# A hand-written order of stages for five queues, replaced by another order of the same stages

## The chip, the cores and the metric

The kernel runs on one core of a Trainium2 chip. The metric is the device time of one execution in microseconds (us); the median of several executions is compared. PE is TensorE (matmuls), DVE is VectorE, ACT is ScalarE, POOL is GpSimd, and SP is the queue that issues every DMA transfer here.

## What is computed

Sliding-window attention with 32 global tokens, then two feed-forward layers in a row, all in float32. Cut to what matters:

```python
# attention: B=4 batches, H=8 heads, 512 local + 32 global tokens, head size 64
s_g = scale * q_g @ concat(k_g, k_l).T          # global queries see everything
out_g = softmax(s_g) @ concat(v_g, v_l)
s_l = concat(q_l @ k_g.T, where(|i - j| <= 32, q_l @ k_l.T, -1e9)) * scale
out_l = softmax(s_l) @ concat(v_g, v_l)
x = concat(out_g, out_l)                        # as 2304 tokens x 512

h = x @ w_in                                    # first FF layer, 512 -> 1024
solu = h * softmax(h)
ln = (solu - mean) / sqrt(var + 1e-6) * g_ln
x = ln @ w_out                                  # 1024 -> 512

h = x @ w_in2                                   # second FF layer, 512 -> 2048
g = where(h >= 1, h, where(h <= -1, 0, (h + 1)**2 / 4))
out = g @ w_out2                                # 2048 -> 512
```

Each float32 matmul of the FF layers is done as three fast ones on a high and a low part of both operands (`mm3`, and `hmm` with its `lo` argument). The weights come as 64-bit words and are turned into these two parts on the chip, in the steps A, C, B, D, F, m, H, L of `conv`.

## The kernel before, in words

The 2304 tokens are 18 tiles of 128 at most; attention and the first FF layer go through 16 tiles of local tokens and one of all global ones, in the order `SEQ`, step by step. The second FF layer follows behind for three blocks of tiles, 16 steps each, and is not touched.

The first eight steps (`SCRIPTED = 8`) are not written as a loop but as one list of short names, `SCRIPT`. A loop takes the names one after the other, and `issue` emits the instructions of each. All five engines are in a manual schedule there, so each engine's queue holds its instructions just in the order of the list; across engines only data, buffers and semaphores set the time. A name is a kind and a step or piece number, and a trailing `v` puts it on DVE in place of ACT or POOL:

- loads, on SP: `q` (qkT, queries and keys of a step), `v` (vw, the value windows), `qg`, `vn` (for the global tokens), `w` (a raw piece of the first layer's weights);
- attention of a step: `S` scores and `G` global scores on PE, `M`, `R`, `Rn` edge mask, row maximum and its scale on DVE, `Ea`, `Eb` exponentials on ACT, `Ta`, `Tb` transposes on PE to pPT and `Pa`, `Pb` their copies, `V` the product with vw on PE (tile o, called pv here), `X` its scaling (xn), `XT` the transposition into the tile xy; `gt`, `gp`, `gv` and so on the same for the global tokens, once in four steps;
- first FF layer of a step: `xh`, `xl` high and low part of x, `ha`, `hA`, `hb`, `hB` the matmuls to h (a step has 24), `mx`, `ex`, `z`, `u`, `bn`, `pw`, `nn` softmax and normalization (`u` is the multiplication e<-e,s,h which reads h a last time), `ta`, `tb`, `tha`, `tla` and so on the transposes to lnT, `ya`, `Ya`, `yb`, `Yb` the matmuls to yT (24 each, for two steps at once);
- weight pieces: `A` to `L`, as above; pieces 16 to 18 belong to the second layer's weights, are stored to memory for later (`s` fetches one, `o` stores one);
- `Z`: three matmuls on a tile of zeros that keep PE occupied (`keep_warm`).

Buffers that bind steps: psH (2 rooms for S and h), psA (3 rooms for transposes, o and others), 2 rooms each for qkT and vw, 3 for raw weights (wraw). A load into a room waits on SP until its last reader is done, and everything behind it on SP waits too.

Behind the list the loop `for p in range(SCRIPTED, NT)` goes on with step 8. Its first pass runs, by `ORDER_1 = "h3x0421g5w"`: h of step 8, the rest of step 11's attention, x of the next step, the transposes of step 12 (pPT), two sets of yT, pv of step 12, and then the scores of step 14.

Of the kernel before, what the change touches and what calls it, by code (L numbers as in the profile page):

```python
# [49 lines left out]
SCRIPTED = 8  # L50

SCRIPT = """
Z0 Z0 Z0 q0 Z0 qg0 w3 q1 A3 w0 S0 M0 Z0 C3 R0 B3 Z0 G0 D3 Gc0 S1 G1 w2 q2 Rn0 M1 F3 Ea0 w5 q3 H3 A0
Ta0 w4 Gc1v R1 Rn1 Eb0 A2 L3 S2 G2 Z0 C0 B0 C2v D0 B2 M2 Ea1 Eb1 F0 A5 C5 I1 D2 H0 R2 Gc2 L0v v0 Z0
Pa0 Tb0 A4 B5 Pb0 F2 G3 w1 H2 Rn2 Ta1 I0 L2 q4 v1 Gc3v qg1 V0 Ea2 C4v gm0 A1 B4 C1 gn0 D4 S3 q5 D5
Tb1 X0 Eb2 M3 R3 B1 Pa1 ge0 Rn3 F4 Z0 F5 Ea3 Z0 Pb1v D1 gt0 XT0 gp0 S4 H4 Ta2 Eb3 M4 L4 V1 gc0 H5
gi0 Tb2 Pa2 w7 L5 R4 Pb2 S5 I2 X1 w6 A7 G4 F1 Rn4 A6 Gc4 M5 Z0 H1 I3 G5 C7v XT1 R5 Z0 Ea4 B7 Gc5 v2
q6 v3 V2 L1 Rn5 xh0 Eb4 X2 C6 Ta3 Pa3v B6 D6 Ea5 Tb3 q7 XT2 S6 w8 F6 Tb4 M6 Pb3 D7 Eb5 Ta4 V3 ha0 H6
xh1 F7 X3 Pa4 Pb4 n0 xl0 L6 R6 A8v w10 H7 L7 G6 v4 Rn6 Gc6 XT3 A10v Ea6 hA0 G7 I4 hb0 q8 Ta5 hB0
Gc7v C10v Eb6 gm1 V4 mx0 C8 B10 ex0 Ta6 I5 xl1 Pa5 ha1 X4 hA1 B8 z0 gn1 D10 D8 I6 w9 F8 Tb5 u0 v5 m8  # L60
hb1 Pb5 F10 V5 XT4 hB1 xh2 bn0 H8 m10 vn0 L8 A9 C9 ge1 v6 mx1 S7 M7 pw0 q9 Pa6 X5 ex1 qg2 Tb6 R7 Pb6
Rn7 xh3 Ea7 w11 Eb7 z1 gv0 B9 H10 go0 gt1 u1 V6 D9 v7 xl2 S8 XT5 nn0 w13 ha2 gp1 X6 M8 R8 L10 A11
xl3 tb0 thb0 ta0 Rn8 tlb0 v8 Ea8 w12 hA2 I7 tha0 C11 Eb8 A13 Tb7 F9 hb2 Ta7 B11 w14 bn1 hB2 tla0 D11
Pa7v xh4 m9 pw1 Pb7 ha3 nn1 C13 tb1 B13 mx2 F11 hA3 qg3 w15 H9 ta1 thb1 tha1 m11 D13 ex2 tlb1 XT6
tla1 L9 z2 F13 H11 s0 hb3 gc1 m13 L11 V7 hB3 Ta8 H13 gi1 mx3 ex3 ya0 Pa8 u2 A12 X7 XT7 bn2 xl4 S9 z3
Tb8 G8 q10 L13 Ya0 A15 xh5 Pb8 M9 u3 ha4 C12 Gc8 A14 G9 Gc9 hA4 R9 C15 Rn9 B15 pw2 q11 G10 C14 B12
B14 D15 D12 Ea9 vn1 nn2 F12 Eb9 m12 H12 F15 yca0 hb4 tb2 I8 hB4 Gc10v ta2 bn3 L12v S10 mx4 V8 m15
D14 xl5 H15 thb2 tlb2 X8 ex4 z4 F14 s1 yb0 tha2 pw3 v9 u4 gv1 tla2 nn3 go1 ha5 s2 m14 M10 G11 Ta9
Pa9v H14 Gc11 R10 bn4 A16 L15 L14 Yb0 v10 ta3 tha3 tb3 hA5 A17v I9 thb3 Tb9 tla3 Rn10 C17 Ea10 hb5
tlb3 ycb0 C16v Ta10 A18 pw4 Eb10 XT8 hB5 ya1 gm2 xh6 mx5 Pb9v ex5 xl6 B16 z5 S11 nn4 u5 bn5 xh7 D16  # L70
M11 V9 B17 Ya1 D17 ha6 gn2 F17 X9 Pa10 F16 Tb10 pw5 Pb10 nn5 tb4 hA6 ta4 tha4 q12 R11 Rn11 yca1 hb6
q13 V10 ge2 yb1 I10 Ea11 xl7v tla4 XT9 thb4v X10 Eb11 tlb4 xd1 hB6 C18 mx6 xh8 B18 Yb1 ex6 z6 S12 u6
tb5 H17 XT10 Ta11 H16 Pa11v M12 thb5 tlb5 ha7 ta5 hA7 tha5v I11 bn6 tla5 ycb1 gt2 R12 Rn12 pw6 hb7
gp2 Ea12 G12 Gc12 gc2 hB7 Eb12 D18 Tb11 L17v ya2 Pb11v G13 nn6 mx7 F18 ex7 S13 Gc13v z7 u7 v11 M13
H18 bn7 L18 R13 L16 Rn13 o0 s3 V11 ta6 tha6 tb6 o1 Ya2 gi2 Ea13 tla6 thb6v Eb13 yca2 vn2 q14 v12
xl8v pw7 tlb6 v13 X11 xd0 I13 I12 nn7
"""

ROOMS = [2, 3, 4, 0, 1, None, None, None, 2, 3, 4, 0, 1, None, None, None]
# [911 lines left out]
```

## Time and profile before

| | |
|---|---|
| median of 3 executions | 704.96 us (704.93 to 706.45) |
| the profiled execution | 709.54 us, of which the span from the first to the last instruction is 707.7 us |
| PE busy in the span | 682.5 us (96%) |
| DVE busy | 421.2 us (60%) |
| ACT busy | 294.4 us (42%) |
| POOL busy | 178.4 us (25%) |
| transfers | 72.25 MB, on the mean 102 GB/s |

The busy shares are means over the whole span, and its parts have different limits. The written list takes PE from 0 to about 168 us, the loop goes on to about 315 us, and the second FF layer takes the rest. So what happens in the list is to be read from windows of the first 170 to 190 us, not from this table. A row of the timeline gives the start, the duration, the engine, the line and the operation with the tile it writes and those it reads, and in brackets how long the engine stood before it and what ended that.

### The profile page before, as it was taken

Reading aid. Unit: us, or ns where it says so; the run is one execution under the profiler, and the core shown is the slowest. Engines: PE = TensorE matmul, PEld = TensorE weight load, DVE = VectorE, ACT = ScalarE, POOL = GpSimd, SP = SyncE. Lnnn points to the kernel's source line nnn. Section 1 sums busy time; section 2 is a strip of 40 time slices with the busy share of each in tenths; the row PEclk is TensorE's granted clock in tenths of the full one; section 3 lists DMA queues with packets and bytes.
Section 4 is the critical chain, followed back from the end, with each engine's and each line's share of the span. In section 5 each row is a group of like instructions: output and inputs, shape, how many; then the busy total and the mean of one; then the engine's idle time right before and its main releaser. Section 6 shows DMA issues by size and latency. Waiting matters only on the chain.

```text
span 707.7 us, 14836 instructions
## 1 busy us (share of the span) xinstructions
PE 682.5 (96%) x6200; PEld 594.5 (84%) x6200; DVE 421.2 (60%) x777; ACT 294.4 (42%) x736; POOL 178.4 (25%) x188
## 2 busy tenths in 40 slices
PE   7889899999799999999999999999999999999997
PEld 3557788888789898899988889899998898999995
DVE  5989898988677569666977774432222243322232
ACT  5876663555346244443444442332222233222222
POOL 2234364103012114202313222222222222222210
PEclk9889999999899999999999999999999999999999
DMA  8978737303932813201322200020000002000002
GB/s 337 359 301 312 286 117 303 110 2 112 370 122 100 298 31 120 60 1 60 119 88 92 90 30 1 2 89 1 1 0 1 1 0 75 16 1 1 0 1 75
DMA packets 18162, 72.25 MB, mean 102 GB/s; under 512 B 2224, under 2 KB 2736, under 8 KB 15536
## 3 DMA queue, kind: packets, MB, share of 16 engines
q1 hardware_dynamic: 18096, 71.32, 27.8%
q8 instruction: 48, 0.79, 0.4%
q14 instruction: 18, 0.15, 0.1%
HBM read 63.71 MB, written 7.60 MB: 101 GB/s over the span
## 4 chain that ended last, share of the span: by engine, by line
PE 70%; DVE 16%; DMA 7%; ACT 4%; issue 3%; SPq 0%; ACTq 0%; DVEq 0%
PE acc L264 21%; PE h L264 20%; PE h L509 9%; PE yT L264 9%; DVE w L177 3%; DVE w L179 2%; PE S L340 2%; DMA wraw<-in_w2i_dram 2%; DMA wraw<-in_w2o_dram 2%; PE plnT L558 2%; PE o L412 2%; DVE nm L137 2%; ACT e L146 2%; DVE xy L137 1%; DMA vw<-in_vwin_dram 1%
## 5 line engine op out<-in xcount | busy, mean ns | idle before, releaser
L264 PE MATMUL h<-yT,w2i 128*128 128x384 f32 (+1 forms) x936 | 167.6, 328 | 2.3 <-DVE xy L137 2.3
L264 PEld LDWEIGHTS h<-yT,w2i 128*128 128x128 f32 x936 | 157.7, 188 | 10.0 <-DVE xy L137 3.8
L161 POOL TENSOR_TENSOR g<-xy,g 128x384 fp32r<-128x384 f32 (+1 forms) x92 | 91.8, 998 | 282.0 <-ACT g L146 262.0
L137 DVE TENSOR_SCALAR xy<-h 128x384 f32<-128x384 f32 (+1 forms) x96 | 51.2, 533 | 145.1 <-PE h L264 128.9
L264 PE MATMUL acc<-w2o,g 128*128 128x512 f32 x510 | 127.9, 394 | 0.0
L146 ACT ACTIVATE xy<-xy 128x384 f32<-128x384 f32 (+1 forms) x96 | 48.4, 504 | 145.8 <-DVE xy L137 145.8
L264 PEld LDWEIGHTS acc<-w2o,g 128*128 128x128 f32 x510 | 94.4, 188 | 17.2
L509 PE MATMUL h<-win,x 128*128 128x512 f32 x408 | 105.5, 405 | 0.4 <-DVE x L497 0.4
L264 PE MATMUL yT<-lnT,wout 128*128 128x256 f32 x768 | 95.1, 281 | 0.7 <-ACT xy L146 0.7
L264 PEld LDWEIGHTS yT<-lnT,wout 128*128 128x128 f32 x768 | 92.1, 188 | 2.1 <-ACT xy L146 0.9
L509 PEld LDWEIGHTS h<-win,x 128*128 128x128 f32 x408 | 74.1, 189 | 17.6 <-issue 1.4
L137 DVE TENSOR_TENSOR xy<-h,xy 128x384 f32<-128x384 f32 (+1 forms) x96 | 51.3, 534 | 56.9 <-ACT xy L146 56.8
L146 ACT ACTIVATE g<-xy 128x384 fp32r<-128x384 f32 (+1 forms) x96 | 48.7, 507 | 60.0 <-DVE xy L137 39.4
L146 ACT ACTIVATE e<-S,nm 128x128 f32<-128x128 f32 x128 | 45.3, 382 | 11.5 <-DVE nm L137 7.7
L264 PE MATMUL h<-yT,lnT 128*128 128x384 f32 (+1 forms) x216 | 38.8, 328 | 0.0
L264 PE MATMUL acc<-lnT,g 128*128 128x512 f32 x153 | 38.2, 393 | 0.0
L264 PEld LDWEIGHTS h<-yT,lnT 128*128 128x128 f32 x216 | 36.5, 188 | 2.0 <-DVE xy L137 0.5
L171 ACT ACTIVATE w<-wraw 128x512 f32<-128x512 f32 x37 | 24.8, 677 | 27.1 <-DMA wraw<-in_w2o_dram 14.6
L264 PEld LDWEIGHTS acc<-lnT,g 128*128 128x128 f32 x153 | 28.3, 188 | 5.1
L177 DVE SCALAR_TENSOR_TENSOR w<-wraw,w 128x512 int32<-128x512 int32 x38 | 32.1, 854 | 0.4
L497 POOL TENSOR_TENSOR x<-xy,x 128x512 fp32r<-128x512 f32 x15 | 20.0, 1335 | 45.3 <-ACT x L146 45.3
L137 DVE TENSOR_REDUCE nm<-h 128x1 f32<-128x1024 f32 x17 | 20.7, 1218 | 17.4 <-PE h L509 17.4
(120 smaller groups left out, 819.2 us busy)
## 6 DMA issues: line engine op xcount, KB each, us to landing
vw<-in_vwin_dram SPq DMA_DIRECT2D x16, 1024.0 KB, 9.6
qkT<-in_qk_dram SPq DMA_DIRECT2D x16, 832.0 KB, 5.2
wraw<-in_w2i_dram SPq DMA_DIRECT2D x16, 512.0 KB, 3.7
wraw<-in_w2o_dram SPq DMA_DIRECT2D x16, 512.0 KB, 3.7
vn<-in_vloc_dram SPq DMA_DIRECT2D x4, 1024.0 KB, 8.1
out_dram<-o SPq DMA_DIRECT2D x16, 256.0 KB, 2.0
xy<-in_w1i_dram SPq DMA_DIRECT2D x5, 512.0 KB, 8.9
xy<-in_w1o_dram SPq DMA_DIRECT2D x5, 512.0 KB, 8.6
```

Source lines behind the costliest of these rows:

```text
L137: self.last = getattr(nc.vector, name)(*args, **kw)
L146: vec.act = nc.scalar.activation(**kw)
L161: eng.tensor_tensor(out=lo, in0=src, in1=hi.bitcast(F32), op=ALU.subtract)
L171: return nc.scalar.activation(out=w.tf, in_=w.high.bitcast(F32), func=AF.Abs)
L177: return nc.vector.scalar_tensor_tensor(out=w.t, in0=w.high, scalar=-0x40000000, in1=w.t, op0=ALU.bitwise_and, op1=ALU.bitwise_or)
L179: return nc.vector.scalar_tensor_tensor(out=w.t, in0=w.low, scalar=29, in1=w.t, op0=ALU.logical_shift_right, op1=ALU.bitwise_or)
L264: mm(out=dst, lhsT=pairs[i][0][x], rhs=pairs[i][1][y], start=start and j == 0, stop=stop and j == 3 * n - 1)
L340: mm(out=S[32 * hp:32 * hp + 32, par, ci], lhsT=qT[r, hp, ci], rhs=kT[r, hp, w:w + 4].rearrange("p c d -> p (c d)"), start=True, stop=True)
L412: mm(out=o[rows, ci, par], lhsT=PT[t][:, par, ci, rows], rhs=w[:, ci, D * h:D * h + D], start=True, stop=True)
L497: eng.tensor_tensor(out=xT[t][1], in0=x[:, :, n:n + P], in1=xT[t][0].bitcast(F32), op=ALU.subtract)
L509: mm(out=hps[t][:, half], lhsT=x[i][:, k], rhs=win[j][:, k, sl], start=not lo and j == 0 and k == 0, stop=lo and k == KD - 1)
L558: nc.tensor.transpose(ps[:, k], ln[t][:, P * c:P * c + P], ident)
```

## The change

`SCRIPT` is written anew. The same stages are in it, with the same numbers, but in another order; `Z` stands there 3 times in place of 12. Some names change the engine by their `v` (for instance `Pa3v` to `Pa3`, `L6` to `L6v`): DVE has 736 rows in the new order and 744 in the old one, PE 2258 and 2314. The loop, the buffers and everything behind the list stay as they were.

```diff
 SCRIPT = """
-Z0 Z0 Z0 q0 Z0 qg0 w3 q1 A3 w0 S0 M0 Z0 C3 R0 B3 Z0 G0 D3 Gc0 S1 G1 w2 q2 Rn0 M1 F3 Ea0 w5 q3 H3 A0
-Ta0 w4 Gc1v R1 Rn1 Eb0 A2 L3 S2 G2 Z0 C0 B0 C2v D0 B2 M2 Ea1 Eb1 F0 A5 C5 I1 D2 H0 R2 Gc2 L0v v0 Z0
...
-H18 bn7 L18 R13 L16 Rn13 o0 s3 V11 ta6 tha6 tb6 o1 Ya2 gi2 Ea13 tla6 thb6v Eb13 yca2 vn2 q14 v12
-xl8v pw7 tlb6 v13 X11 xd0 I13 I12 nn7
+qg0 q0 w2 S0 w1 q1 M0 A2 w0 G0 C2 q2 R0 B2 Rn0 w3 D2 A1 v0 Ea0 Eb0 C1 F2 H2 w7 S1 B1 D1 L2 Gc0 Ta0
+F1 I0 A0 M1 C0 Pa0 Tb0 S2 R1 G1 B0 q3 D0 Rn1 H1 Pb0 A3 Ea1 Z0 Gc1 F0 C3 M2 V0 R2 B3 Rn2 H0 Ta1 D3 w6
...
+Eb12 Gc13v G12 H16 Gc12 S13 Tb11 Pb11 ya2 mx7 V11 nn6 tb6 L16v M13 ta6 vn2 R13 ex7 Rn13 z7 Ea13 tha6
+H18 xd1 u7 xl8 o0 Eb13 thb6 bn7 pw7 Ya2 L18 v13 nn7 s3 I13 o1 yca2 q14 XT10 tlb6 X11 gi2 I12 tla6
 """
```

Three places show what moved. The first is SP's queue at the end of the list, which feeds the loop's first pass. Before, from the vw of step 11 (vw_2697) to the vw of steps 12 and 13 (vw_2808 and vw_2813); w2d_i0 and w2d_i1 are the stores `o0` and `o1`, wraw_2715 is the fetch `s3`, vg and vn are `vn2`, qkT_2806 is `q14`:

```order
L318 DMA vw_2697<-in_vwin_dram 128x2048
L245 DMA w2d_i0_2713<-wraw_1545 128x1024
L233 DMA wraw_2715<-in_w2o_dram 128x1024
L245 DMA w2d_i1_2761<-wraw_1931 128x1024
L323 DMA vg_2803<-in_vglo_dram 32x512
L324 DMA vn_2802<-in_vloc_dram 128x2048
L314 DMA qkT_2806<-in_qk_dram 128x1664
L318 DMA vw_2808<-in_vwin_dram 128x2048
L318 DMA vw_2813<-in_vwin_dram 128x2048
```

Now, from the vw of step 11 (vw_2272) on; vw_2558 is that of step 12, vw_2766 that of step 13, qkT_2776 is `q14`:

```order
L317 DMA vw_2272<-in_vwin_dram 128x2048
L313 DMA qkT_2538<-in_qk_dram 128x1664
L317 DMA vw_2558<-in_vwin_dram 128x2048
L322 DMA vg_2704<-in_vglo_dram 32x512
L323 DMA vn_2703<-in_vloc_dram 128x2048
L244 DMA w2d_i0_2726<-wraw_1924 128x1024
L317 DMA vw_2766<-in_vwin_dram 128x2048
L232 DMA wraw_2769<-in_w2o_dram 128x1024
L244 DMA w2d_i1_2773<-wraw_1926 128x1024
L313 DMA qkT_2776<-in_qk_dram 128x1664
L313 DMA qkT_2834<-in_qk_dram 128x1664
```

The vw of step 12 moved from behind both stores to a place ahead of them and of vg and vn; the one of step 13 stands between the stores, and q14 is still behind the second.

The second place is PE's queue at the first matmul to h, the first work of the FF layer. Before, with the last of twelve keep-warm sets ahead of it:

```order
L270 MATMUL Z<-zero 128x512
L412 MATMUL o<-vw,PT 32x64 x32
L397 MATMUL pPT<-ident,e 128x128 x8
L340 MATMUL S<-qkT 32x128 x32
L397 MATMUL pPT<-ident,e 128x128 x8
L412 MATMUL o<-vw,PT 32x64 x32
L509 MATMUL h<-win_133,x 128x512 x4
L509 MATMUL h<-win_134,x 128x512 x4
```

Now:

```order
L269 MATMUL Z<-zero 128x512
L339 MATMUL S<-qkT 32x128 x32
L396 MATMUL pPT<-ident,e 128x128 x4
L411 MATMUL o<-vw,PT 32x64 x32
L396 MATMUL pPT<-ident,e 128x128 x4
L508 MATMUL h<-win_133,x 128x512 x4
L508 MATMUL h<-win_134,x 128x512 x4
```

Before, seven scores, six global scores, ten half transposes, four pv (o) and the transposes of the first global group stand ahead of the first h, with all twelve keep-warm sets; now five scores, four global scores, six half transposes and two pv, with three sets. The difference stands behind it.

The third place is DVE's queue at the end of the list, from the row maximum of h of step 7 (nm<-h) to the multiplication `u7` (e<-e,s,h), which frees the room of h. Before, with the normalization of step 6 (e<-e,mv,rstd) ahead of it:

```order
L137 TENSOR_SCALAR e_2457<-e_2457,mv,rstd 128x1024
L137 TENSOR_REDUCE nm_2653<-h 128x1
L179 SCALAR_TENSOR_TENSOR w_2131<-wraw,w_2131 128x512
L137 COPY Sg<-G 128x128 x2
L137 TENSOR_SCALAR s_2657<-s_2657 128x1
L137 RECIPROCAL s_2657<-s_2657 128x1
L137 SCALAR_TENSOR_TENSOR e_2656<-e_2656,s_2657,h 128x1024
```

Now:

```order
L136 TENSOR_REDUCE nm_2655<-h 128x1
L136 TENSOR_SCALAR e_2385<-e_2385,mv,rstd 128x1024
L184 TENSOR_TENSOR wraw<-w_1973,wraw 128x512
L136 TENSOR_TENSOR S<-S,masks 128x8x2x32
L136 TENSOR_REDUCE nm<-S 128x8
L136 TENSOR_SCALAR nm<-nm 128x8
L136 TENSOR_SCALAR s_2710<-s_2710 128x1
L136 RECIPROCAL s_2710<-s_2710 128x1
L136 STREAM_TRANSPOSE xy_90<-ogn 128x4x32
L136 SCALAR_TENSOR_TENSOR e_2709<-e_2709,s_2710,h 128x1024
```

The normalization of step 6, a low part of a weight piece (wraw), the mask and the row maximum of step 13 and a transposition moved in between; a weight step and the copies to Sg moved ahead.

## Rows read from the trace of the kernel before

**Rows 1.** Stretches: us, busy PE, PEld, DVE, ACT, POOL (instructions), clock, DMA share, GB/s.

```profile
0.00:48.98 48.98, 39.38 (x918) 23.63 (x919) 36.46 (x76) 34.75 (x135) 13.39 (x27) 0.86 0.85 327
48.98:76.27 27.29, 24.98 (x511) 18.51 (x507) 25.62 (x49) 18.63 (x59) 12.72 (x12) 0.96 0.91 346
76.27:168.20 91.93, 91.39 (x1343) 78.20 (x1340) 82.94 (x158) 48.11 (x147) 31.61 (x32) 0.99 0.37 136
184.85:190.40 5.55, 5.55 (x153) 5.00 (x153) 2.90 (x5) 0.66 (x3) 0.00 (x0) 0.52 0.97 356
```

**Rows 2.** Timeline of PE around the end of the list (start, duration, operation).

```profile
162.32 1.16 PE L340 MATMUL S<-qkT 64*32 64x128 f32 x64
163.41 1.10 PE L412 MATMUL o<-vw,PT 128*32 128x64 f32 x64
164.44 1.09 PE L558 MATMUL plnT<-ident,e 128*128 128x128 f32 x8
165.29 3.07 PE L264 MATMUL yT<-lnT,wout 128*128 128x256 f32 x24
168.20 2.03 PE L509 MATMUL h<-win,x 128*128 128x512 f32 x8
...
175.28 5.89 PE L264 MATMUL yT<-lnT,wout 128*128 128x256 f32 x48
184.85 1.93 PE L412 MATMUL o<-vw,PT 128*32 128x64 f32 x64 [3.68 <-DMA vw<-in_vwin_dram]
186.72 1.96 PE L340 MATMUL S<-qkT 64*32 64x128 f32 x64
...
189.03 1.60 PE L558 MATMUL plnT<-ident,e 128*128 128x128 f32 x8
```

**Rows 3.** Timeline of SP's queue around the end of the list.

```profile
132.23 0.33 SPq L318 DMA_DIRECT2D vw<-in_vwin_dram  x1
166.43 0.33 SPq L245 DMA_DIRECT2D w2d_i<-wraw  x1
171.39 0.33 SPq L233 DMA_DIRECT2D wraw<-in_w2o_dram  x1
...
174.43 0.99 SPq L318 DMA_DIRECT2D vw<-in_vwin_dram  x2
```

**Rows 4.** Timeline of POOL around the end of the list.

```profile
163.87 2.54 POOL L185 TENSOR_TENSOR wraw<-w,wraw 128x512 fp32r<-128x512 f32 x2 [0.17 <-ACT wraw L146]
```

**Rows 5.** Chain of work that ended last, in order of time (start, us, what).

```profile
174.43 10.29 DMA vw<-in_vwin_dram
```

**Rows 6.** Groups by line and shape, 0 to 190 us: busy, mean ns, idle before.

```profile
L137 DVE TENSOR_REDUCE nm<-S 128x8 f32<-128x1024 f32 x15 | 18.2, 1215 | 0.1
...
L137 DVE TENSOR_TENSOR S<-S,masks 128x512 f32<-128x512 f32 x15 | 10.4, 691 | 10.7 <-PE S L340 10.7
...
L179 DVE SCALAR_TENSOR_TENSOR w<-xy,w 128x512 int32<-128x512 int32 x10 | 6.7, 673 | 0.0
...
L173 DVE TENSOR_SCALAR w<-w 128x512 f32<-128x512 f32 x5 | 2.0, 410 | 0.2 <-ACT w L171 0.2
...
L137 DVE TENSOR_TENSOR xn<-o,rs 128x512 f32<-128x512 f32 x13 | 8.8, 676 | 5.8 <-PE o L412 5.8
...
L270 PE MATMUL Z<-zero 128*128 128x512 bf16 x36 | 13.9, 510 | 1.5 <-DVE zero L303 1.2
```

**Rows 7.** DMA issues: count, KB each, median us from issue to landing.

```profile
qkT<-in_qk_dram SPq DMA_DIRECT2D x16, 832.0 KB, 5.2
...
vw<-in_vwin_dram SPq DMA_DIRECT2D x16, 1024.0 KB, 9.6
...
xy<-in_w1i_dram SPq DMA_DIRECT2D x5, 512.0 KB, 8.9
```

**Rows 8.** Timeline of DVE near the end of the list.

```profile
160.02 0.79 DVE L137 TENSOR_SCALAR e<-e,mv,rstd 128x1024 f32<-128x1024 f32 x1
...
162.56 0.49 DVE L137 COPY Sg<-G 128x128 f32<-128x128 f32 x2
...
163.69 1.28 DVE L137 SCALAR_TENSOR_TENSOR e<-e,s,h 128x1024 f32<-128x1024 f32 x1
```

More of the change, by code (lines that the diff above doesn't have):

```diff
@@ L52 @@
 SCRIPT = """
-Z0 Z0 Z0 q0 Z0 qg0 w3 q1 A3 w0 S0 M0 Z0 C3 R0 B3 Z0 G0 D3 Gc0 S1 G1 w2 q2 Rn0 M1 F3 Ea0 w5 q3 H3 A0
-Ta0 w4 Gc1v R1 Rn1 Eb0 A2 L3 S2 G2 Z0 C0 B0 C2v D0 B2 M2 Ea1 Eb1 F0 A5 C5 I1 D2 H0 R2 Gc2 L0v v0 Z0
-Pa0 Tb0 A4 B5 Pb0 F2 G3 w1 H2 Rn2 Ta1 I0 L2 q4 v1 Gc3v qg1 V0 Ea2 C4v gm0 A1 B4 C1 gn0 D4 S3 q5 D5
-Tb1 X0 Eb2 M3 R3 B1 Pa1 ge0 Rn3 F4 Z0 F5 Ea3 Z0 Pb1v D1 gt0 XT0 gp0 S4 H4 Ta2 Eb3 M4 L4 V1 gc0 H5
-gi0 Tb2 Pa2 w7 L5 R4 Pb2 S5 I2 X1 w6 A7 G4 F1 Rn4 A6 Gc4 M5 Z0 H1 I3 G5 C7v XT1 R5 Z0 Ea4 B7 Gc5 v2
@@ L58 @@
[L58 to L72, printed above, removed]
@@ L73 @@
-tb5 H17 XT10 Ta11 H16 Pa11v M12 thb5 tlb5 ha7 ta5 hA7 tha5v I11 bn6 tla5 ycb1 gt2 R12 Rn12 pw6 hb7
-gp2 Ea12 G12 Gc12 gc2 hB7 Eb12 D18 Tb11 L17v ya2 Pb11v G13 nn6 mx7 F18 ex7 S13 Gc13v z7 u7 v11 M13
-H18 bn7 L18 R13 L16 Rn13 o0 s3 V11 ta6 tha6 tb6 o1 Ya2 gi2 Ea13 tla6 thb6v Eb13 yca2 vn2 q14 v12
-xl8v pw7 tlb6 v13 X11 xd0 I13 I12 nn7
+qg0 q0 w2 S0 w1 q1 M0 A2 w0 G0 C2 q2 R0 B2 Rn0 w3 D2 A1 v0 Ea0 Eb0 C1 F2 H2 w7 S1 B1 D1 L2 Gc0 Ta0
+F1 I0 A0 M1 C0 Pa0 Tb0 S2 R1 G1 B0 q3 D0 Rn1 H1 Pb0 A3 Ea1 Z0 Gc1 F0 C3 M2 V0 R2 B3 Rn2 H0 Ta1 D3 w6
@@ new lines @@
+L1 L0v Eb1 A7 X0 qg1 Ea2 Pa1 C7 XT0 xh0 G2 S3 B7 q4 Tb1 Gc2v F3 Eb2 v1 G3 D7 Z0 A6 M3 Z0 xl0 R3 w4
+Gc3v Rn3 C6 F7 gm0 S4 B6 Pb1 gn0 w5 H3 Ea3 H7 M4 I1 Ta2 R4 D6 Eb3 V1 Tb2 ge0 I2 F6 X1 L3 A4 v2 L7
+Pa2 Rn4 C4 H6 B4 A5 C5 Ea4 Pb2v XT1 ha0 gt0 D4 gp0 B5 Ta3 q5 hA0 Eb4 D5 F4 Tb3 F5 V2 L6v H4 H5 L4v
+v3 L5v S5 Pa3 X2 v4 hb0 M5 gi0 R5 I4 w10 Rn5 hB0 XT2 n0 mx0 xh1 Pb3 G4 I3 V3 Ea5 Gc4 X3 Ta4 XT3 Tb4
+ex0 Pa4 xl1 z0 u0 q6 w8 Pb4 G5 Gc5v V4 Eb5 q7 S6 bn0 A10 M6 gc0 R6 X4 ha1 pw0 C10 Rn6 A8 G6 hA1 xh2
@@ new lines @@
+B10 Gc6 w9 G7 Ea6 hb1 nn0 I5 Gc7 D10 ta0 F10 Ta5 vn0 Eb6 gm1 m10 hB1 S7 tha0 tla0 Pa5 H10 Tb5 v5 tb0
+q8 A9 L10 C9 xh3 mx1 ex1 M7 gn1 Pb5 gv0 R7 z1 Rn7 thb0 qg2 u1 go0 tlb0 XT4 vn1 C8 V5 xl2 S8 Ea7 Eb7
+Ta6 w14 ge1 Pa6 bn1 xl3 B8 pw1 X5 M8 D8 v6 Tb6 ha2 Pb6 w11 nn1 gt1 hA2 tb1 hb2 R8 Rn8 thb1v B9 q9
+gp1 I6 V6 F8 tlb1 Ta7 Ea8 Eb8 XT5 D9 F9 hB2 w12 A11 m8 ha3 X6 G9 Pa7 hA3 m9 w13 H9 v7 Tb7 XT6 C11v
+B11 Gc9v mx2 H8 w15 v8 ta1 hb3 D11 L9 Pb7v Ta8 F11 hB3 tha1 ex2 xh4 gi1 gc1 z2 tla1 V7 Tb8 u2 mx3
@@ new lines @@
+xh5 m11 I7 H11 L8 S9 A12 L11 A13 X7 M9 C12 ya0 Pa8 ex3 bn2 G8 A14 C13 xl5 pw2 z3 R9 B12 qg3 I8 q10
+C14 u3 B14 Ya0 xl4 ha4 Pb8 nn2 D14 V8 Gc8v B13 D13 hA4 tb2 hb4 Rn9 ta2 D12 Ea9 F14 F12 thb2 F13 q11
+hB4 bn3 Eb9 m12 tlb2 tha2 XT7 X8 mx4 m13 m14 H12 L12 ha5 G10 H14 tla2 A15 xh6 pw3 yca0 C15 Gc10 hA5
+gv1 ex4 Ta9 B15 H13 Tb9 s0 s1 D15 z4 go1 L13v F15 m15 u4 hb5 L14v yb0 Pa9 A16 H15 G11 C16 Pb9v v9
+L15 S10 q12 B16 nn3 Yb0 ta3 M10 R10 Gc11 s2 bn4 Rn10 tb3 A17 tha3 tla3 thb3 tlb3 I9 hB5 mx5 D16 ycb0
@@ new lines @@
+Ea10 V9 ya1 xh7 XT8 Ta10 Ya1 ex5 pw4 z5 C17v Eb10 xl6 gm2 u5 F16 A18 Pa10 ha6 gn2 S11 Tb10 hA6 nn4
+v10 X9 tb4 v11 C18v Pb10 hb6 xd0 ta4 yca1 bn5 hB6 B18 tha4 thb4 M11 V10 R11 yb1 pw5 B17 nn5 XT9 Rn11
+mx6 Ea11 I10 tlb4 tla4 D17 F17 ex6 D18 Ta11 ge2 Yb1 z6 u6 xh8 H17 S12 L17 X10 tb5 bn6 Pa11v pw6 Eb11
+M12 ha7 thb5 ycb1 gt2 xl7 R12 tlb5 gp2 Rn12 hA7 ta5 I11 tha5v hb7 gc2 q13 G13 tla5 Ea12 F18 v12 hB7
+Eb12 Gc13v G12 H16 Gc12 S13 Tb11 Pb11 ya2 mx7 V11 nn6 tb6 L16v M13 ta6 vn2 R13 ex7 Rn13 z7 Ea13 tha6
```

## The prediction

> **What bounds the kernel now.** Three views were read in turn. First the busy times by stretch, because the change stays inside the written list, which PE leaves at 168.20 us. From 76.27 us to there PE is busy 91.39 of 91.93 us, and from 48.98 to 76.27 us 24.98 of 27.29 [rows 1]. So from its first h matmul on, at 48.98 us, the end of the list is PE's own work; ahead of it PE fills in (39.38 us busy, 36 keep-warm matmuls with 13.9 us among them [rows 6]) and DVE, with 36.46 of 48.98 us, and the transfers, at 327 GB/s, carry the chains that lead to it [rows 1].
>
> Then PE's rows at the seam between list and loop. The loop's first h starts at 168.20 us, its yT pair at 175.28 us, and then PE stands 3.68 us and the transfer of a vw tile ends that wait at 184.85 us. [...]
>
> Last, why that vw was late: the chain has it under way for 10.29 us, from 174.43 us [rows 5]. SP issued nothing between 132.23 us and 166.43 us. It stood at the stash store "w2d_i<-wraw" until POOL had ended the two "wraw" subtractions (163.87 us plus 2.54 us) [rows 3, 4]; the next stash fetch needs the room of that store and follows at 171.39 us, and behind it stand vn, qkT and the two vw of 174.43 us [rows 3]. Who waits for the first of them, v12, is PE's pv of step 12, the fourth stage of the loop's first pass.
>
> **The seam: what the change does to it.** In the new list v12 stands ahead of vn2 and of the store o0, and only v13, q14 and the stash moves are behind o0. What v12 waits for in the new place is the room of v10, freed when PE has done V10; behind V10 PE still has four sets of 24 yT matmuls (half of the pair's 5.89 us each) and 24 of h (8 take 2.03 us) before the seam [rows 2], some 17 us, against the 10.29 us of the slow transfer [rows 5]. The stall goes with what follows from it: 3.68 idle, plus 0.83 for o, 0.80 for S and 0.51 for plnT at the lower clock [rows 2], 5.8 us in all. What is late next: q14 is wanted by S of step 14, behind h, pPT, yT and pv of the loop's first pass. o0 now waits for a subtraction on DVE instead of POOL; in DVE's queue it stands ahead of M, R and the multiplication of the tail (below), some 3.5 us, and 1 us of slack, so 4.5 us ahead of the seam. The fetch s3 follows a store later, 171.39 - 166.43 = 4.96 us [rows 3], and q14 right behind; with the 5.2 us in which a qkT lands [rows 7] it is there some 6 us after the seam, and S stood more than 16 us behind the first h before (184.85 - 168.20 [rows 2]), of which 13 us remain without the stall. So S finds it. Of the 5.8 us I take all; the bounds are 3.7 (the stall goes, but another low-clock stretch comes) and 5.8.
>
> **The list up to the first h.** Of DVE's instructions nothing new comes ahead of the first h, and these fall behind it: 2 edge masks, 1 row maximum, 4 of the short weight steps (1 B, 3 C), 3 of the long ones (2 D, 1 F), and 1 each of xn, its transpose and a PT copy. With 0.69, 1.22, 0.41, 0.67 and 0.68 us [rows 6] (B taken as C, D as F, transpose and copy as xn, whose 512 columns they share; instructions on eight columns or so left out) that is 1.38 + 1.22 + 1.64 + 2.01 + 2.04 = 8.3 us. Against it stands the start: q0 is issued behind qg0, 0.3 us (an issue of SP takes 0.33 [rows 3]), and without the twelve matmuls that ran ahead of it S0 runs at the lower clock, 1.96 against 1.16 us [rows 2], 0.8 more. So the first h comes 8.3 - 1.1 = 7.2 us sooner, if DVE sets it.
>
> But PE then has more left: 2 S, 2 G, 4 half transposes, 2 pv and one gtrans, which ran ahead of the first h, now run behind it. By the distances of the starts in [rows 2] S takes 1.09, pv 1.03, a set of eight transposes 0.85 us, and G, with a quarter of S's matmuls, 0.27. That is 2 x 1.09 + 2 x 1.03 + 2 x 0.85 + 1.06 (ten transposes) + 2 x 0.27 = 7.6 us. As PE is busy from the first h to the end, this is added to the end: the list ends 7.6 - 7.2 = 0.4 us later. The keep-warm matmuls taken out (27 of 36) cost nothing and give nothing by themselves, since all lay ahead of the first h, where PE waited in between; two sets of three, right ahead of that h, did hold up work, but for PE these are moments before it is the bound.
>
> Bounds of this part. Were it the transfers that set the first h, then 3 qkT of 832 KB, one weight piece of 512 KB and one vw of 1024 KB fewer ahead of it [rows 7] are 4.0 MB, at 327 GB/s [rows 1] 12.3 us, and the list would end 7.6 - 12.3 = -4.7 us, so 4.7 us sooner. [...] I take 0.4, because DVE was busy for three quarters of that stretch, while the last transfer which the first h needs, that of v0, had been issued long before (it is the tenth of SP's queue).
>
> **The tail of the list.** On DVE the row maximum and mask of step 13 and the normalization of step 6 now stand ahead of the multiplication u7, whose end frees the PSUM room that the loop's first h writes. Before, u7 ended at 164.97 us [rows 8], 3.2 us ahead of that h at 168.20 us [rows 2]. Added between are M 0.69, R 1.22 and a subtraction of 0.68 [rows 6] and the normalization, 0.79 [rows 8], taken out are a weight step of 0.67 [rows 6] and a copy of 0.49 us [rows 8]: 2.2 us more, so 1.0 us is left. I cost it at nothing; where DVE lags by more than before, each us of lag beyond 1.0 is one on PE.
>
> **Sum.** +0.4 for the list and -5.8 for the seam give -5.4 us. Behind it nothing moves: the loop and the FF stages have the same instructions in the same order, and PE is busy nearly all the time there, so the gain is carried to the end. The profiled execution takes 709.54 us; it would take 704.1. The median of the runs is 4.6 us shorter than the profiled one, and I take off the same: 704.96 - 5.4 = 699.6 us.
>
> **Rivals.**
> 1. *Transfers set the early part.* The list ends 4.7 us sooner, and with the seam 10.5 us: 694.5 us. For it: the DMA share is 0.85 up to 48.98 us and 0.91 up to 76.27 us [rows 1]. Against it: counted to the third h tile instead of the first, in the same way, 6.3 us of DVE's instructions fall behind and 5.7 us come ahead, so the head start may be spent by then.
> 2. *The wait moves on.* The loop's first h waits for u7, or S of step 14 for q14, which is still behind o0, and eats most of the 5.4 us; the PE pause lowers the clock again. With 1 us of low-clock cost and 4 us of wait: 704.6 us. For it: only 1.0 us of slack on DVE. Against it: DVE's queue is eight instructions shorter over the whole list, and the S wait has some 6 us of reserve.
> [...]
>
> That the change does nothing is no case: the five queues are written by hand from the list, and their order is different from the first row on.
>
> **How the numbers follow.** The forecast (699.6, with 697 to 702.8 as its own range, from the seam's 3.7 to 5.8 and from DVE's bound of a few us) gets 0.46, rival 1 (694.5) 0.18, rival 2 (704.6) 0.16, rival 3 (708.2) 0.20. About 0.3%, 2.1 us, is what a measurement of this kernel can tell from no change, so faster is the forecast and rival 1: 0.64. Rival 2 is the same: 0.16. Slower is rival 3: 0.20. The range goes from 693.5, just beyond rival 1, to 708.0, which leaves about half of rival 3 out and keeps the rest.
>
> **What would show it.** Right: in the changed profile the loop's first pass has no PE wait for vw and the clock stays up there; v12 is issued well ahead of the stash store. The first h starts near 42 us (48.98 - 7.2) and PE reaches the loop's first h at 168 to 169 us. [...] Wrong altogether would be a PE that stands in the stretch from the first h to the seam, because a step's inputs come later than its place in the list; PE hardly waits there now, and nothing in the trace of before can show whether the new order keeps that.

## The result, and the profile after

The new order takes 696.0 us (median of 4, 695.27 to 696.97) against 704.94 (median of 4, 701.5 to 706.45): ratio 0.988, interval 0.984 to 0.992, so 8.9 us faster. A second timing gave 698.35 against 704.51, ratio 0.990 (0.987 to 0.993). The forecast was 699.6 us, 693.5 to 708.0.

The page of the profiled execution after (695.27 us, span 693.3 us), and two windows of it, up to the first h and from there to the loop's first h, which answer to [rows 1]:

```profile
PE 669.4 (97%) x6173; PEld 590.0 (85%) x6173; DVE 417.6 (60%) x772; ACT 297.2 (43%) x741; POOL 175.2 (25%) x188
...
0.00:34.17 34.17, 21.92 (x562) 15.42 (x562) 24.27 (x49) 24.99 (x92) 13.74 (x28) 0.95 0.90 343
34.17:161.21 127.04, 123.41 (x2178) 102.09 (x2177) 118.72 (x233) 80.56 (x262) 39.58 (x43) 1.00 0.62 232
```

The first h stands at 34.17 us, not 48.98; the loop's first h at 161.21, not 168.20. PE's timeline after at the seam answers to [rows 2] (start, duration, operation):

```profile
161.21 5.76 PE L508 MATMUL h<-win,x 128*128 128x512 f32 x24
166.80 1.04 PE L396 MATMUL pPT<-ident,e 128*128 128x128 f32 x8
167.59 5.90 PE L263 MATMUL yT<-lnT,wout 128*128 128x256 f32 x48
173.43 1.10 PE L411 MATMUL o<-vw,PT 128*32 128x64 f32 x64
174.46 1.16 PE L339 MATMUL S<-qkT 64*32 64x128 f32 x64
...
175.76 1.09 PE L557 MATMUL plnT<-ident,e 128*128 128x128 f32 x8
176.61 3.75 PE L508 MATMUL h<-win,x 128*128 128x512 f32 x15
```

Nothing stands in brackets: PE waits for no vw, and o, S and plnT are at 1.10, 1.16 and 1.09 us, where they were at 1.93, 1.96 and 1.60 (granted clock 1.00 from 173.43 to 176.85 us, 0.52 before [rows 1]). SP's queue says why, beside [rows 3]:

```profile
136.06 0.33 SPq L317 DMA_DIRECT2D vw<-in_vwin_dram  x1
...
154.93 0.33 SPq L244 DMA_DIRECT2D w2d_i<-wraw  x1
157.57 0.33 SPq L317 DMA_DIRECT2D vw<-in_vwin_dram  x1
```

The vw of step 12 is issued at 136.06 us, 37 us ahead of its use; the store goes out 6.3 us ahead of the loop's first h (161.21 - 154.93), before 1.8 (168.20 - 166.43). From the loop's first h to the next step's first h PE takes 15.4 us (161.21 to 176.61), before 22.2 (168.20 to 190.39). I call this the seam's step.

In this pair the span fell by 14.4 us (707.7 to 693.3): 7.0 by the loop's first h, 6.8 in the seam's step, 0.6 behind. That is more than the medians show, since the profiled execution of before lay 4.6 us above its median. So two questions are left: is the seam worth its 6 us in the timed runs too, and what took 7 us off the list in this pair, where 0.4 more was forecast?

### The profile page after: what moved, and what is told of

It is laid out like the page before. It is cut to its first block, busy times and chain, and to the rows that moved or that the text cites. A ratio compares the mean times of both kernels' runs of the same rounds, so it can differ in the third digit from the quotient of the medians.

```text
span 693.3 us, 14782 instructions
## 1 busy us (share of the span) xinstructions
PE 669.4 (97%) x6173; PEld 590.0 (85%) x6173; DVE 417.6 (60%) x772; ACT 297.2 (43%) x741; POOL 175.2 (25%) x188
## 4 chain that ended last, share of the span: by engine, by line
PE 77%; DVE 10%; DMA 8%; ACT 2%; issue 2%; POOL 0%; SPq 0%; ACTq 0%; DVEq 0%
PE h L263 23%; PE acc L263 23%; PE h L508 11%; PE yT L263 10%; DMA wraw<-in_w2o_dram 3%; DMA qkT<-in_qk_dram 2%; DMA wraw<-in_w2i_dram 2%; PE S L339 2%; PE o L411 2%; DVE w L178 2%; PE plnT L557 2%; DVE w L176 2%; PE pPT L396 2%; DMA vw<-in_vwin_dram 1%; DVE nm L136 1%
## 5 line engine op out<-in xcount | busy, mean ns | idle before, releaser
L263 PE MATMUL h<-yT,w2i 128*128 128x384 f32 (+1 forms) x936 | 167.5, 327 | 1.6 <-DVE xy L136 1.6
L496 POOL TENSOR_TENSOR x<-xy,x 128x512 fp32r<-128x512 f32 x17 | 22.2, 1314 | 45.4 <-ACT x L145 45.4
L339 PE MATMUL S<-qkT 64*32 64x128 f32 x1024 | 21.4, 300 | 11.2 <-DMA qkT<-in_qk_dram 11.1
L543 POOL TENSOR_TENSOR rstd<-rstd,nhalf 128x1 f32<-128x1 f32 x17 | 10.4, 611 | 79.1 <-DVE rstd L136 72.6
```

The costliest lines, as they stand in the source:

```text
L263: mm(out=dst, lhsT=pairs[i][0][x], rhs=pairs[i][1][y], start=start and j == 0, stop=stop and j == 3 * n - 1)
L339: mm(out=S[32 * hp:32 * hp + 32, par, ci], lhsT=qT[r, hp, ci], rhs=kT[r, hp, w:w + 4].rearrange("p c d -> p (c d)"), start=True, stop=True)
L496: eng.tensor_tensor(out=xT[t][1], in0=x[:, :, n:n + P], in1=xT[t][0].bitcast(F32), op=ALU.subtract)
```

## Experiments

Every kernel is an edit of one of the two lists, but for one added stage. Old kernels are compared with the kernel before on the same chip (704.3 to 706.2 us), new ones with each other and with the new order (696.0 and 698.35).

### The old order with v12 alone moved

```diff
-... Rn13 o0 s3 V11 ... q14 v12
+... Rn13 v12 o0 s3 V11 ... q14
```

> The kernel before with one name moved: v12 stands ahead of o0 instead of behind q14. Theory (the seam stall comes from the load of v12 standing behind the stash store on SP): PE no longer waits for vw at the seam, the clock stays up there, the time falls by about 5.8 us to about 699. Rival (the wait moves on: vn2, q14 or the row of stash moves is late next): PE waits elsewhere within the first two passes of the loop, and the time falls by less than 2 us.

Measured: 702.78 us against 704.34, ratio 0.997 (0.994 to 1.000). PE's timeline of this kernel at the seam:

```profile
170.19 2.03 PE L509 MATMUL h<-win,x 128*128 128x512 f32 x8
...
177.27 5.89 PE L264 MATMUL yT<-lnT,wout 128*128 128x256 f32 x48
183.09 1.10 PE L412 MATMUL o<-vw,PT 128*32 128x64 f32 x64
184.12 1.16 PE L340 MATMUL S<-qkT 64*32 64x128 f32 x64
...
186.28 3.98 PE L509 MATMUL h<-win,x 128*128 128x512 f32 x16
```

The wait is gone, and the step takes 16.1 us (186.28 - 170.19). But the loop's first h came only at 170.19, 2.0 us later than before, although the two programs are alike up to that load. A second timing was to show which number holds:

> The kernel before with the load v12 alone moved ahead of the store o0, a second time. Theory A (the seam's wait costs the 4 to 6 us that the traces show, and the first timing of 1.6 to 2.1 us came out low by chance): 3 to 5 us faster than before. Theory B (the pauses in which PE waits for nothing shown, earlier in the list, and the seam's wait absorb each other, so that less than the wait is won): 0.5 to 3 us faster.

Measured: 698.95 us against 706.22, ratio 0.991 (0.987 to 0.994). The step took 16.1 us again, but the loop's first h now stood at 163.49 us. The same program differs by 6.7 us in its list from one execution to the other. The two ran on two chips, but one chip is enough for such a spread: on the chip of the second timing the runs of the kernel before lie between 700.56 and 710.0 us. The wait went as the first expectation had it, but not the 5.8 us; the 7.3 us of the second timing (706.22 - 698.95) lie beyond both ranges. The step is 4 to 6 us shorter in both traces than with the wait, and something else moves the list by as much from one execution to the next.

### The new order with the seam undone, in two steps

```diff
-... F18 v12 hB7 ... ta6 vn2 R13 ... L18 v13 nn7 s3 I13 o1 yca2 q14 XT10 ...
+... F18 hB7 ... ta6 R13 ... L18 nn7 s3 I13 o1 vn2 q14 v12 v13 yca2 XT10 ...
```

> The new order with the loads at the end of the list put back: vn2, q14, v12 and v13 stand behind the second stash store o1 again, all else is as in the new order. Theory A (the seam is worth what its rows say): PE waits for vw in the loop's first pass and the clock falls behind it, so this kernel is 4 to 6 us slower than the new order, and keeps 3 to 5 us of gain over the kernel before, all of it from the front of the list. Rival (the seam is worth only the 2 us that the load of v12 gave when it was moved alone in the old order): 1 to 3 us slower than the new order.

Measured: 696.59 us (ratio to before 0.989, 0.986 to 0.991), no slower than the new order's 698.35. Theory and rival both fell. SP's queue shows the reason: the store is early, and so is all that stands behind it.

```profile
156.20 0.33 SPq L244 DMA_DIRECT2D w2d_i<-wraw  x1
...
161.98 1.04 SPq L317 DMA_DIRECT2D vw<-in_vwin_dram  x2
```

The vw went out 0.5 us ahead of the loop's first h (162.48), 12.7 ahead of its use. In the new list the subtraction L16, which the store waits for, is on DVE (`L16v`) and early. The second step took this back too:

```diff
-... tb6 L16v M13 ... u7 xl8 o0 ... Ya2 L18 nn7 ...
+... tb6 M13 ... u7 xl8 L18 L16 o0 ... Ya2 nn7 ...
```

> As the new order with vn2, q14, v12 and v13 behind the second stash store, and now also with the subtraction that the first store waits for (L16) back on POOL, behind L18, right ahead of that store. Theory A (two changes in the new order each take the seam's wait away: v12's place, and the store's input being early on DVE): the store is issued near 165 us in place of 156, the vw of step 12 near 170, PE waits 4 to 7 us for it behind the yT pair, the clock falls after that, and the total is 4 to 9 us above the new order. Theory B (the new list's end has no such wait in it, since the loads are early in any case): no wait, total within 1 us of the new order.

Measured: 705.65 us against 706.22 of before, ratio 1.000 (0.998 to 1.003): the whole gain is gone. SP's queue and PE's timeline of this kernel:

```profile
166.37 0.33 SPq L244 DMA_DIRECT2D w2d_i<-wraw  x1
...
172.07 1.02 SPq L317 DMA_DIRECT2D vw<-in_vwin_dram  x2
```

```profile
163.83 5.76 PE L508 MATMUL h<-win,x 128*128 128x512 f32 x24
...
182.15 1.94 PE L411 MATMUL o<-vw,PT 128*32 128x64 f32 x64 [6.01 <-DMA vw<-in_vwin_dram]
184.01 1.71 PE L339 MATMUL S<-qkT 64*32 64x128 f32 x64
...
186.80 5.85 PE L508 MATMUL h<-win,x 128*128 128x512 f32 x24
```

The step takes 23.0 us (186.80 - 163.83), 7.6 more than in the new order; the time is 7.3 us above the new order's 698.35 (9.7 above 696.0), which was timed on another chip. By the ratios to before (1.000 and 0.990) it is 7 us as well. So the seam is worth all that was timed here, and two edits of the new list each take its wait away.

### Keep-warm matmuls

Four kernels: without the two sets right ahead of the first h (old order; the diff), without any (old, then new order), and with four more sets at the very start of the new list:

```diff
-... Gc4 M5 Z0 H1 I3 G5 C7v XT1 R5 Z0 Ea4 ...
+... Gc4 M5 H1 I3 G5 C7v XT1 R5 Ea4 ...
```

> The kernel before without the last two keep-warm sets, those right ahead of the first h. Theory A (those two sets, 2.9 us at the low clock, stood in PE's own path to the first h): the first h starts 3 to 5 us sooner and the time falls by 2.5 to 4 us. Theory B (the prediction's step: all keep-warm work lies in moments in which PE would wait anyway): within 1 us of the kernel before. Rival (the clock falls without them): the first h runs at about 0.5 of the clock and the time rises by 2 us or more.

> The kernel before without any keep-warm set. Theory A: as without the last two, 2.5 to 4 us less, since the other ten lie where PE waits. Theory B: no change. Rival (cold start, each early S 0.8 us and each pv 0.83 us longer): 3 us or more above the kernel without the last two.

> The new order without its three sets of keep-warm matmuls (Z). Theory A (in the new order PE has enough work of its own in front, and Z only fills waits): the first h within 0.7 us of 34.2, total within 1.5 us of the new order. Theory B (the cold start counts, as it did in the old order, where all Z taken out cost 6 to 7 us): S, pPT and pv ahead of the first h run at the lower level, first h 2 to 4 us later, and the total 2 to 6 us longer.

> The changed kernel with four keep-warm sets put back at the very start, ahead of the first scores, as the kernel before had them. If the cold start costs what the prediction took for it (0.8 us on the first S, and more on the tiles behind it), S0 takes 1.16 instead of 1.96 us and the time falls by 0.8 us or more; if the early part is held by the transfers of qkT, nothing changes (within 0.7 us).

Measured: two sets fewer gave 706.17 us, ratio 1.002 (0.999 to 1.005), so nothing; the first h came at 48.22 us. All twelve fewer gave 711.35, ratio 1.008 (1.005 to 1.011), 7 us slower: its first 8 h matmuls take 3.78 us, before 2.13, and the loop's first h comes at 172.94. In the new order none at all gave 697.50, ratio to before 0.989, the same as with three sets (698.35), though the first h came at 35.27 us, 1.1 to 1.5 later. Four sets at the start gave 700.61, ratio to before 0.994 (0.992 to 0.997): no gain. Its first S took 1.16 us, where it takes 1.96 in the new order, but its first h (34.19) came no sooner, and its seam's step (15.4 us) is as in the new order. Part of what it lost in its profile lies in the loop, where PE waits 1.97 us for DVE at 277.41 us with a plnT; why is open.

### More work on DVE in front

```diff
+            elif kind == "K":
+                for _ in range(5):
+                    vec.tensor_tensor(out=spare, in0=spare, in1=spare, op=ALU.mult)
```

The new stage stands ahead of M2 in one kernel and behind XT0 in the other.

> The new order with five more DVE instructions of 128x512 (some 0.6 us each, 3.0 us in all, on a tile that nobody else reads) ahead of M2, the edge mask that ran at 18.1 us; the result is not touched. Theory A (DVE sets the front: it never stands between 12 us and the first h but for 1.1 us, and the rooms of the loads are freed behind its work): first h 2 to 3 us later, the loop's first h and the total 2 to 3 us later. Theory B (the transfers set the front): first h later by at most 1 us, total within 1 us.

> The new order with the same five extra DVE instructions (3.0 us) a little later: behind XT0, the transposition of the first x, which ran at 22.6 us. What frees the room of the fifth qkT (X0, then G2 on PE) is then ahead of them. Theory A (DVE's work ahead of X0 counts, since that chain feeds the load that S4 waits for; behind it there is slack): first h later by at most 1 us, total later by 0 to 1.5 us. Theory B (every us of DVE in front counts alike): first h, loop's first h and total 2 to 4 us later, as with the extra work ahead of M2.

The five instructions took 5 us, not 3; DVE's row in the first kernel, and what PE waited for up to 38 us there (us in total, times, longest):

```profile
18.84 4.97 DVE L136 TENSOR_TENSOR spare<-spare 128x512 f32<-128x512 f32 x5
```

```profile
PE S L341 <- DMA qkT<-in_qk_dram: 8.6, 2, 6.4
PE G L385 <- DVE xn L136: 6.9, 1, 6.9
```

Measured: ahead of M2, first h at 37.77 us (3.6 later than 34.17), loop's first h at 167.63, 700.3 us in all, 2.0 above the new order on the same chip. Behind XT0, where I had expected slack, first h at 36.56 (2.4 later), loop's first h at 166.43, 699.65 us, which is 1.3 and 3.7 above the two medians of the new order. So DVE is on the path to the first h of the new order, with its work ahead of X0 and behind it, though of 5 us only 3.6 and 2.4 arrive there. In the first of these kernels a score waits for its qkT, but as PE's G waits for xn on DVE first, and the room of a qkT comes free only when S and G have read it, that load is late because DVE is; the DMA share is 0.73 up to 34.00 us, where in the new order it is 0.90 up to 34.17.

### The two kernels once more

> The new order once more, without an edit, so that its parts can be measured beside it on one chip. Ratio to the kernel before 0.986 to 0.992. Theory A (the order of the queues sets the early part): the first h at 34.2 us, the loop's first h near 161 us, as in its first profile, give or take 0.5 us. Theory B (what moved those two by 7 us more than forecast was the chance of one execution, such as the pauses in which PE waits for nothing the profile shows): they lie elsewhere by 2 us or more in this execution.

> The kernel before without an edit, one more profiled execution. If the places that the comparison rests on are those of the kernel and not of one execution: first h at 48 to 49.5 us, the loop's first h at 166 to 170.5, a wait for vw of 2 to 4 us at the seam, and pauses without a reason shown at the same matmuls of PE's queue (near the 600th and the 1360th), of other lengths.

The new order took 698.35 us. First h at 33.75 us and loop's first h at 162.71, so the front held, and the seam lay 1.5 later, between what the two theories had. The old one: first h at 48.68, loop's first h at 168.96, a vw wait of 3.33 us, 707.97 us. Its pauses, PE rows whose idle time ends with "issue" (PE waited for nothing that the profile shows), beside those of other kernels:

Before:

```profile
37.16 1.70 PE L340 MATMUL S<-qkT 64*32 64x128 f32 x50 [2.52 <-issue]
74.40 1.94 PE L340 MATMUL S<-qkT 64*32 64x128 f32 x58 [1.53 <-issue]
```

Before, once more:

```profile
36.91 1.71 PE L340 MATMUL S<-qkT 64*32 64x128 f32 x50 [2.93 <-issue]
...
75.21 1.10 PE L340 MATMUL S<-qkT 64*32 64x128 f32 x58 [2.85 <-issue]
```

Old order with v12 moved, first execution, then the second:

```profile
75.61 1.94 PE L340 MATMUL S<-qkT 64*32 64x128 f32 x58 [4.29 <-issue]
```

```profile
71.32 1.10 PE L340 MATMUL S<-qkT 64*32 64x128 f32 x58 [0.94 <-issue]
```

Old order with two keep-warm sets fewer:

```profile
72.97 1.17 PE L340 MATMUL S<-qkT 64*32 64x128 f32 x52 [1.74 <-issue]
```

New order, first and second execution:

```profile
64.95 0.53 PE L411 MATMUL o<-vw,PT 128*32 128x64 f32 x20 [0.46 <-issue]
```

```profile
66.90 0.53 PE L411 MATMUL o<-vw,PT 128*32 128x64 f32 x20 [1.00 <-issue]
```

All pauses of PE from the start to the loop's first h, added up from the timelines (us; the difference is the loop's first h less the pauses; kernels of the old order first):

| kernel | loop's first h | pauses | difference | seam's step |
|---|---|---|---|---|
| before | 168.20 | 4.59 | 163.6 | 22.2 |
| before, once more | 168.96 | 7.36 | 161.6 | 21.0 |
| old, two sets fewer | 166.75 | 5.24 | 161.5 | 20.2 |
| old, v12 moved | 170.19 | 9.23 | 161.0 | 16.1 |
| old, v12 moved, second | 163.49 | 3.55 | 159.9 | 16.1 |
| new order | 161.21 | 0.46 | 160.8 | 15.4 |
| new order, second | 162.71 | 1.44 | 161.3 | 15.4 |
| new, no keep-warm | 163.47 | 1.39 | 162.1 | 15.4 |
| new, four sets at the start | 163.19 | 2.14 | 161.0 | 15.4 |
| new, loads back | 162.48 | 0.79 | 161.7 | 15.4 |
| new, loads and L16 back | 163.83 | 1.27 | 162.6 | 23.0 |

Three kernels are not in the table: the two with more DVE work, and the old order without keep-warm matmuls, whose loop's first h came at 172.94 us with 7.56 us of pauses (difference 165.4), so that pauses may have a part in its 7 us too.

The five old executions have a mean of 167.5 us and 6.0 us of pauses, the six new ones 162.8 and 1.2. Less the pauses the means are 161.5 and 161.6, with 159.9 to 163.6 in single executions: so far as these show, the list itself takes the same time in both orders. In the pair of old executions that are one program (v12 moved), the list differs by 6.7 us and the pauses by 5.7. This is arithmetic on profiled executions and no run in which the pauses were taken away; that they are what made the new list shorter in these profiles fits the numbers, and is not shown by an edit.

## Why the prediction was right, point by point

**The seam, -5.8: right in mechanism, and near in size.** The step went from 22.2 to 15.4 us, 6.8 less in the pair, 1.0 beyond the upper bound; o, S and plnT gave back the 0.83, 0.80 and 0.51 us of [rows 2], with the granted clock at 1.00 in place of 0.52, and besides a G (0.68 to 0.48) and a wait of 0.4 us for x inside the h of the old order. In the three other executions of the old order with the wait it was 4.8, 5.3 and 5.6 more than 15.4. In timed runs it is 1.6 and 7.3 us (v12 moved in the old order) and 7.3 (both edits undone in the new one). The vw of step 12 went out 25 us ahead of the seam (136.06 to 161.21), where I had counted some 17. What I did not see is that L16 on DVE would have been enough: I had the store going out 4.5 us ahead of the seam, it went 6.3, and with that even the loads behind it are in time. The tail cost nothing, as forecast: the first h of the loop has no wait in front of it.

**The list, +0.4: this is the term that was mis-sized.** It measured -7.0 in the pair and -4.7 on the mean of the executions above. In the timed runs less of it is left: with 4.8 to 6.8 us for the seam, 2.1 to 4.1 of the first timing's 8.9 us, and between 0.6 lost and 1.4 won of the second's 6.2 (704.51 - 698.35). That the medians came out 3.6 and 1.25 us below the forecast is this term and the seam's spread together; which had what share the runs do not say. The first h came 14.8 us sooner, not 7.2. By arithmetic 12.2 of this is DVE's busy time ahead of it (36.46 to 24.27), where I counted 8.3. I had counted all DVE work whose name stands ahead of `ha0`; but in the new order the first h started, at 34.17 us, while some 3 us of that work was still to come on DVE, since it needs none of it: a weight step, xn, a PT copy and a transposition, in DVE's timeline after.

```profile
34.39 0.64 DVE L178 SCALAR_TENSOR_TENSOR w<-wraw,w 128x512 int32<-128x512 int32 x1
34.95 0.68 DVE L136 TENSOR_TENSOR xn<-o,rs 128x512 f32<-128x512 f32 x1
...
35.95 0.68 DVE L136 COPY PT<-pPT 128x512 f32<-128x512 f32 x1
36.55 0.70 DVE L136 STREAM_TRANSPOSE xy<-xn 128x512 f32<-128x512 f32 x1
```

Another 2.5 us is the pause of before at 37.16 us. Behind the first h PE took 7.8 us more (127.04 against 119.22), close to the 7.6 forecast (its terms add up to 7.5), but by luck: before had 2.1 us of pauses in this stretch and after 0.46, so less these the stretch grew by 9.4. What was left out altogether is the pauses. They stood in the trace of before, 4.6 us up to the seam, and I read the stretch as PE's own work.

**That DVE and not the transfers sets the front** is half shown. The two runs with more DVE work put DVE on the path. But up to 34.17 us PE waits 10.7 us for qkT in the new order and 0.5 for xn, and the last of these loads lies on the chain to the first h (from the chain and from PE's timeline):

```profile
23.09 5.82 DMA qkT<-in_qk_dram
```

```profile
29.05 1.64 PE L339 MATMUL S<-qkT 64*32 64x128 f32 x64 [1.59 <-DMA qkT<-in_qk_dram]
```

It was issued when G had read the room, and G had waited 0.52 us for xn on DVE: DVE's work and a transfer's time follow each other there. I had put the transfers aside because v0, to my mind the last load that the first h needs, goes out early; but S of step 4 stands ahead of that h in PE's queue, and its qkT goes out only at 23.09 us. Rival 1 is as near in its numbers as the forecast, in the profile nearer: it had 12.3 us for the first h, and 14.8 less the pause of 2.5 is 12.3; from its terms follow a first h near 37 us (48.98 - 12.3) and a seam near 164 (168.20 - 4.7), and it had 694.5 us in all. No run loaded the transfers alone, so how much of the front is theirs stays open.

**Keep-warm matmuls** taken out gave nothing by themselves: right for the two sets ahead of the first h, and for the last three of the new order. No run shows the 708.2 us of **rival 3**: with its three sets the new order took 696.0 us, three of the five S ahead of its first h 1.96 us each and the other two 1.15 and 1.64, and its first 8 h matmuls 2.11, at a granted clock of 0.95 up to 34.17 us and 1.00 from there to 36.30. Nor is the lower clock, to which I had put the 0.8 us of the first S, in the trace: that S took 1.96 us as forecast, but at a granted clock of 1.00 (6.13 to 7.80 us). All sets taken out cost 7 us in the old order, of which 1.65 are seen at its first 8 h matmuls (3.78 against 2.13), and nothing in the new one: there the first 8 h matmuls take 2.11 us at 35.27, the mean granted clock of that execution is 0.999, and the 1.1 to 1.5 us by which they came later are not seen in the total. **Rival 2** did not happen: S of step 14 and the loop's first h find their inputs.

## What to carry to other kernels

A wait at the seam of two schedules can be worth its whole price, the slow matmuls behind it (granted clock 0.52 in the kernel before) with it (7.3 us in two of three timings here, 1.6 in the third), but more than one edit may remove it: to price it, undo all of them. What stands ahead of a milestone is what its operands need and what its own engine's queue holds before it, not all that a list writes before it. Add up the idle time without a shown releaser before a bound is called "PE's own work", and take a second profile of the kernel before: here one program ended its list 6.7 us apart in two executions, on two chips.

## What was not expected of the hardware

PE pauses at fixed places of its queue, in the middle of a row of equal matmuls that all have their inputs: with 50 and with 58 scores of a step left in the old order, at 20 pv left in the new one. With six matmuls fewer ahead of it the second pause came with 52 scores left in place of 58, so it is bound to the position in the queue and not to the data. Counted by PE's weight loads, one to a matmul, both orders have their pauses on one and the same grid: the longest of the old order come 604 and 1367 into the queue, those of the new one at 477 and 1240, where the old one has some too, and others, in one order or the other, at 731, 858, 985, 1113, 1620, 1874 and 2001: multiples of 127 matmuls apart, to within two, in the thirteen of fourteen executions that have such pauses. So taking out 36 matmuls ahead (the old order without keep-warm) or 9, or adding 12 (the new order) left the count and moved the pause within the stage: at 604 it came with 19 scores left in place of 50, at 1240 with 10 and 32 pv in place of 20. Off the grid are one of 0.8 us at 194 in four executions of the old order, and five of 0.16 to 0.33 us at keep-warm matmuls. At most places of the grid no pause shows. The length changes from one execution to the next: 0.94, 1.53, 1.74, 2.85 and 4.29 us at the same place. In the old order that place falls into a stretch with the transfers at full load; in the new one the place at 65 us falls where they are nearly still. Stretches of the old order with v12 moved, of before, and of the new order:

```profile
71.32:75.61 4.29, 0.01 (x1) 0.00 (x0) 2.55 (x3) 1.71 (x4) 3.52 (x3) 0.77 1.02 410
```

```profile
72.87:74.40 1.53, 0.00 (x1) 0.00 (x1) 1.53 (x4) 1.53 (x7) 0.43 (x1) 0.89 1.01 418
```

```profile
64.00:65.00 1.00, 0.54 (x37) 0.38 (x29) 1.00 (x2) 0.94 (x5) 1.00 (x1) 1.00 0.14 51
```

The last but one number is the DMA share: 1.02 and 1.01 against 0.14. But a full load alone does not make a pause long: at 477 in the new order's second execution it is 0.44 us at a share of 0.95 (30.90 to 31.35 us).

The pauses on the grid up to the loop's first h come to 2.8 to 7.9 us of a list of 165 in the old order. No run took the transfers away at such a place, so the cause is left open, and also why the new order has shorter pauses.
